# Attention, then two gated feed-forward layers, on one core: fewer filler matmuls in the prologue, and one tile's normalisation split between two engines

## The chip, the core and the metric

One core of a Trainium2 chip runs the whole program in one launch. The metric is device time in microseconds (us) of one execution; lower is better. TensorE (PE) does the matmuls, VectorE (DVE), ScalarE (ACT) and GpSimd (POOL) the work on elements, SyncE's queue (SP) issues nearly all transfers (DMA).

## What is computed

```python
# attention: q, k, v [4, 8, 768, 64], 8 memory keys a head, chunks of 32, 16 left and 8 right
scores = scale * q_c @ concat(mem_k, k_ctx)^T        # 32 x up to 64
a = exp(scores - max); a = a / (sum(a) + 1e-9)
out[chunk] = a @ concat(mem_v, v_ctx)
x = out as [3072, 512]
x = (sigmoid(x @ w_gate) * (x @ w_val)) @ w_out      # d_ff 1536
h = x @ w_in                                         # d_ff 2048
y = (h * sigmoid(1.702 h)) @ w2_out                  # [3072, 512]
```

Inputs and weights are wider than 32 bits where they are weights of the layers; each is converted to a high and a low 32-bit part on the chip, and every layer matmul is done as three (high x high, high x low, low x high).

## The kernel before, in words

Attention is cut into 32 tiles of 96 tokens (three chunks of 32); the layers run over blocks of 512 tokens. The first six tiles (`NPRO` = 6, t = 0 to 5) feed the first block and form the **prologue**: nothing else can be multiplied until their output is there. Each tile goes through the same steps: transposes of q and k on PE (L397, L405), their eviction on ACT (L412, L417, L418), the scores S on PE (L508), maximum and subtraction on DVE (L525, L528), exp on ACT (L536), sum, addition of 1e-9 and reciprocal on DVE (L565, L567, L568), the normalisation (L576: three bands of 32 rows by 448 and one piece of 96 by 64 for the memory keys, written into `pw`), the transpose PT on PE (L598) and its eviction on ACT (L605), the product PV with v on PE (L655), and the split of its result into the high part `xh` on ACT (L687) and the low part `xl` on DVE (L690). In the same stretch the first weights are converted, one unit u at a time: load (L262), rebias on ACT (L266), shift, sign and join on DVE or ACT (L271, L280 or L276, L285), high part on ACT (L290), low part on DVE or GpSimd (L295).

The order of all instructions is made ahead by a planner (`Schedule`): each task has an engine, a planned duration and a due time, and the planner lists tasks in order of planned start. Every engine then works through its own list strictly in order, waiting on semaphores. Only the order is fixed by the plan; on the chip the durations are what they are.

When the planner's list is emitted, `run` puts **filler matmuls** ahead of every PE task of the prologue: wherever the plan has PE waiting, `int(FILL * gap / FILL_US)` products of the identity with itself (L809, 128x128, float32, result never read) are queued, from the time `WAKE` up to the first product of the first layer (L745, `sch.first`). Their number is fixed in the program: they are run whether PE really has to wait at that place or not.

The first layer's products are L745 (high parts) and L752 (low part), with the gate at L769 to L780 and the second matmul at L924; the second layer's are L1231 and L719. After the prologue `open_late` gives the prologue's memory to later buffers: the spare weight buffers `raw_s` and the q and k buffer of tiles 6 to 8 (`qkn_a`) lie there, so their loads wait until the prologue's last reader is done, the fillers' identity tile included.

The normalisation's engines stand in `en` (L590): one name for each of the three bands, and the memory piece goes with band 0. In the kernel before, tiles 0, 2 and 4 have all pieces on GpSimd, the other tiles have band 0 and the memory piece on DVE and two bands on GpSimd.

Of the kernel before, what the change touches and what calls it, by code (L numbers as in the profile page):

```python
# [24 lines left out]
TK = TQ + LEFT + RIGHT  # L25
NEG = -1.0e30
HOP = 0.2
WAKE, FILL, FILL_US = 1.4, 0.8, 0.107
SAME = 0.05


# [92 lines left out]
def c_dve(n, k=1):  # L124
    return k * 0.13 + n / 960.0


def c_act(n):
    return 0.13 + n / 1200.0
# [7 lines left out]
def kernel(  # L137
# [35 lines left out]
    NPRO = len(tiles[0])  # L173
# [179 lines left out]
    def attention(t, bufs, banks, pe_path, extra=None):  # L353
# [9 lines left out]
        def tadd(eng, dur, fn, r=(), w=(), **kw):  # L363
            add(eng, dur, fn, r=r, w=w, slack=SL, **kw)
# [207 lines left out]
        def norm(eng, dst, rows_, keys):  # L572
            r = slice(*rows_)
            c = slice(*keys)
            n = rows_[1] - rows_[0]
            eng.tensor_tensor(  # L576
                out=dst, in0=e3()[r, :, c], in1=T["sm"][r].to_broadcast([n, H, keys[1] - keys[0]]), op=ALU.mult
            )

        if pe_path:  # L580

            def ev_norm(c):
                r = (c * CH, (c + 1) * CH)
                eng = nc.vector if en[c] == "dve" else nc.gpsimd
                norm(eng, T["pw"][r[0] : r[1], :, c * CH : c * CH + CTX], r, (0, CTX))

            def ev_norm_m():
                norm(nc.vector if en[0] == "dve" else nc.gpsimd, T["pw"][:, :, TK:P], (0, TQ), (CTX, KW))

            en = ["pool", "pool", "pool"] if t < NPRO and t % 2 == 0 else ["dve", "pool", "pool"]  # L590
            for c in range(NCK):
                tadd(en[c], 0.75 if en[c] == "dve" else 1.2, lambda c=c: ev_norm(c), r=ke + [kk["sm"]], w=[(kk["pw"], c)])
            tadd(en[0], 0.25 if en[0] == "dve" else 0.35, ev_norm_m, r=ke + [kk["sm"]], w=[(kk["pw"], 3)])

            def pe_pt():
                for h in range(H):
                    a, p = divmod(h, NP)
                    nc.tensor.transpose(  # L598
                        bt[a][:, p * TQ : (p + 1) * TQ], T["pw"][:, h, :], ident()[:TQ, :TQ]
                    )  # L600

            def ev_pt(a):
                src = bt[a][:, : NP * TQ]
                dst = T["pt"].rearrange("p (a h) s -> p a (h s)", a=2)[:, a, :]
                nc.scalar.activation(dst, src, AF.Copy)  # L605

            tadd("pe", 0.7, pe_pt, r=[(kk["pw"], c) for c in range(4)] + [bufs.kid], w=kbt, margin=mg)
            for a in range(2):
                tadd("act", c_act(384), lambda a=a: ev_pt(a), r=[kbt[a]], w=[(kk["pt"], a)])
        else:  # L610

            def ev_norm():
                norm(nc.vector, T["pn"][0:L, :, 3 * CH - NM : 3 * CH], (0, L), (CTX, KW))
                norm(nc.vector, T["pn"][L:TQ, :, CTX:KW], (L, TQ), (CTX, KW))

            tadd(
                "pool",
                0.95,
                lambda: norm(nc.gpsimd, T["pn"][:, :, 0:CTX], (0, TQ), (0, CTX)),
                r=ke + [kk["sm"]],  # L620
                w=[(kk["pn"], 0)],
            )
            tadd("dve", c_dve(128, 2), ev_norm, r=ke + [kk["sm"]], w=[(kk["pn"], 1)])


            PTB = ((0, 0, 0), (1, 0, 1), (2, 0, 2), (0, 1, 1), (1, 1, 2), (2, 1, 3), (0, 2, 3), (1, 2, 3))

            def ev_pt(part):
                for c, kb, r in PTB[4 * part : 4 * part + 4]:
                    nc.vector.transpose(  # L630
                        T["pt"][r * CH : (r + 1) * CH, :, c * CH : (c + 1) * CH],
                        T["pn"][c * CH : (c + 1) * CH, :, kb * CH : (kb + 1) * CH],
                    )

            for part in range(2):
                tadd(
                    "dve",
                    c_dve(1024, 4),
                    lambda part=part: ev_pt(part),
                    r=[(kk["pn"], 0), (kk["pn"], 1)],  # L640
                    w=[(kk["pt"], part)],
                )
# [224 lines left out]
    def attend(ts, bufs, banks):  # L867
        for t in ts:
            attention(t, bufs(t), banks(t), True)
# [37 lines left out]
    def attention_b(b):  # L907
        for t in tiles[b]:
            if t < NPE:
                continue  # L910
            first = t == NPE
            x = pb[(t // 2) % 2 * 2 + t % 2]
            head = first or t % 2 == 0
            attention(t, x, (A0, A1), False, (0 if head else NCK, 2 - t % 2 if head else 0, first or t % TPB == 0))
# [474 lines left out]
```

## Time and profile before

| | |
|---|---|
| median of 3 runs | 1194.86 us (1193.78 to 1195.18) |
| the profiled execution | 1193.88 us, of which its span is 1192.1 us |
| PE busy | 1184.7 us, 99% of the span |
| DVE, ACT, POOL busy | 716.7, 474.7, 80.9 us |
| granted TensorE clock | 1.00 of full speed (2.4 GHz) in every slice |

Matmul records overlap: the sum of durations of a group counts time twice, so the time that a run of matmuls took is read from the chain of work or from start to start. One float32 matmul leaves two records (two passes). "x44" in a row on fillers is thus 22 fillers. Rows are read as start, length, what, count.

### The profile page before, as it was taken

The numbers are of one execution on the slowest core, as the hardware profiler recorded it, in microseconds if no ns is written. First come the engines' busy times: TensorE is split into PE (matmuls) and PEld (weight loads), VectorE is DVE, ScalarE is ACT, GpSimd is POOL, SyncE is SP. The second block draws the span as 40 slices with busy tenths as digits, with TensorE's granted clock in tenths as the row PEclk, the third lists the DMA queues.
The fourth block names the chain that finished last, engine by engine and source line by source line (L and its number), as shares of the span: only waits on it lengthen the run. The fifth ranks groups of instructions, "written<-read, shape, count | busy, mean of one in ns | idle before, by whom it ended". The sixth has DMA issues, their size and how long they took to land.

```text
span 1192.1 us, 19585 instructions
## 1 busy us (share of the span) xinstructions
PE 1184.7 (99%) x7574; PEld 995.2 (83%) x7574; DVE 716.7 (60%) x1465; ACT 474.7 (40%) x832; POOL 80.9 (7%) x82
## 2 busy tenths in 40 slices
PE   9999999999999999999999999999999999999998
PEld 8878889998888888888888888888888888888887
DVE  5699847885478347716874788857333356253342
ACT  4688732222122212212253686746233344243332
POOL 4323310000000000000000100000000000000000
PEclk9999999999999999999999999999999999999999
DMA  9386332233123202301272347645243453244100
GB/s 210 98 251 200 100 79 48 51 58 82 20 47 58 56 17 48 68 14 26 72 258 78 124 148 246 216 159 168 71 124 89 124 150 115 69 126 116 44 36 35
DMA packets 193484, 122.09 MB, mean 102 GB/s; under 512 B 138480, under 2 KB 159216, under 8 KB 193392
## 3 DMA queue, kind: packets, MB, share of 16 engines
q1 hardware_dynamic: 189936, 114.56, 35.3%
q10 hardware_dynamic: 3456, 6.29, 1.4%
q8 instruction: 59, 0.97, 0.4%
q14 instruction: 33, 0.27, 0.1%
HBM read 93.54 MB, written 27.26 MB: 101 GB/s over the span
## 4 chain that ended last, share of the span: by engine, by line
PE 98%; DMA 1%; DVE 0%; ACT 0%; issue 0%; POOL 0%; DVEq 0%; POOLq 0%
PE bank L719 22%; PE bank L745 22%; PE bank L1231 19%; PE bank L924 17%; PE bank L752 11%; PE bank L809 3%; PE bank L655 2%; PE bank L508 2%; DMA raw<-in_moe_w_val_dram 1%; PE bank L598 1%; PE bank L405 0%; PE bank L397 0%; DMA raw_s<-in_moe_w_gate_dram 0%; DVE f L285 0%; ACT sig L769 0%
## 5 line engine op out<-in xcount | busy, mean ns | idle before, releaser
L1231 PE MATMUL bank<-sb_x,sb_r 128*128 128x512 f32 x1008 | 241.0, 389 | 0.0
L745 PE MATMUL bank<-xh,w 128*128 128x512 f32 (+1 forms) x656 | 234.0, 365 | 0.6 <-ACT sig L769 0.5
L745 PE MATMUL bank<-xl,w 128*128 128x512 f32 (+1 forms) x656 | 232.9, 363 | 0.0
L1231 PEld LDWEIGHTS bank<-sb_x,sb_r 128*128 128x128 f32 x1008 | 189.2, 188 | 39.3
L719 PE MATMUL bank<-w,gh 128*128 128x512 f32 x672 | 206.8, 389 | 0.0
L924 PE MATMUL bank<-gh,w 128*128 128x512 f32 (+1 forms) x656 | 158.8, 364 | 0.0
L752 PE MATMUL bank<-xh,w 128*128 128x512 f32 (+1 forms) x656 | 158.3, 366 | 0.0
L719 PEld LDWEIGHTS bank<-w,gh 128*128 128x128 f32 x672 | 126.2, 188 | 26.2
L745 PEld LDWEIGHTS bank<-xh,w 128*128 128x128 f32 x656 | 123.8, 189 | 21.1 <-ACT sig L769 1.2
L745 PEld LDWEIGHTS bank<-xl,w 128*128 128x128 f32 x656 | 123.8, 189 | 19.4
L924 PEld LDWEIGHTS bank<-gh,w 128*128 128x128 f32 x656 | 115.0, 189 | 19.7 <-ACT f L944 0.2
L752 PEld LDWEIGHTS bank<-xh,w 128*128 128x128 f32 x656 | 114.0, 189 | 20.2
L719 PE MATMUL bank<-w,gl 128*128 128x512 f32 x336 | 130.7, 389 | 0.0
L772 DVE SCALAR_TENSOR_TENSOR sig<-sig,bank 128x512 f32<-128x512 f32 (+1 forms) x82 | 50.8, 619 | 106.7 <-PE bank L752 106.1
L777 ACT ACTIVATE gh<-sig 128x512 fp32r<-128x512 f32 (+1 forms) x82 | 47.6, 580 | 161.9 <-DVE sig L772 161.9
L769 ACT ACTIVATE sig<-bank 128x512 f32<-128x512 f32 (+1 forms) x82 | 44.8, 546 | 126.1 <-PE bank L752 123.6
L1247 DVE TENSOR_TENSOR sb_s<-bank,sb_s 128x512 f32<-128x512 f32 x72 | 49.5, 691 | 72.3 <-PE bank L1231 60.4
L630 DVE STREAM_TRANSPOSE pt<-raw 32x256 f32<-32x256 f32 x184 | 80.0, 435 | 2.4
L924 PE MATMUL bank<-gl,w 128*128 128x512 f32 (+1 forms) x328 | 80.7, 368 | 0.0
L719 PEld LDWEIGHTS bank<-w,gl 128*128 128x128 f32 x336 | 63.1, 188 | 13.1
L1243 ACT ACTIVATE sb_s<-bank 128x512 f32<-128x512 f32 x72 | 43.1, 599 | 68.6 <-PE bank L1231 64.7
L1274 ACT ACTIVATE sig<-sb_s 128x512 f32<-128x512 f32 x72 | 45.5, 632 | 59.3 <-DVE sb_s L1247 38.0
(126 smaller groups left out, 1322.4 us busy)
## 6 DMA issues: line engine op xcount, KB each, us to landing
sb_r<-wc_dram SPq DMA_DIRECT2D x112, 256.0 KB
raw<-in_moe_w_out_dram SPq DMA_DIRECT2D x24, 512.0 KB
wc_dram<-sb_r SPq DMA_DIRECT2D x24, 512.0 KB
raw<-in_moe_w_in_dram SPq DMA_DIRECT2D x16, 512.0 KB
y_dram<-f ACTq DMA_DIRECT2D x24, 256.0 KB
out_dram<-f SPq DMA_DIRECT2D x23, 256.0 KB
vn<-in_v_dram SPq DMA_DIRECT2D x24, 240.0 KB
f<-in_q_dram SPq DMA_DIRECT2D x276, 16.0 KB
```

The costliest lines, as they stand in the source:

```text
L630: nc.vector.transpose(T["pt"][r * CH : (r + 1) * CH, :, c * CH : (c + 1) * CH], T["pn"][c * CH : (c + 1) * CH, :, kb * CH : (kb + 1) * CH],)
L719: nc.tensor.matmul(ps_out, a, c, start=(first and i == 0 and j == 0), stop=(last and i == n - 1 and j == 2),)
L745: nc.tensor.matmul(bank[bk][:, :n], w[:, 0, ts[t]], x[xb][:, t, c0 : c0 + n], start=t == 0 and x is xhs, stop=False)
L752: nc.tensor.matmul(bank[bk][:, :n], w[:, 1, ts[t]], xhs[xb][:, t, c0 : c0 + n], start=False, stop=t == NK - 1)
L769: nc.scalar.activation(sig[:, :n], bank[src_sig][:, :n], AF.Tanh, scale=scale / 2)
L772: nc.vector.scalar_tensor_tensor(out=sig[:, :n], in0=sig[:, :n], scalar=1.0, in1=bank[src_val][:, :n], op0=ALU.add, op1=ALU.mult)
L777: nc.scalar.activation(gh[:, :n], sig[:, :n], AF.Copy, scale=0.5)
L924: nc.tensor.matmul(bank[Y[m]][:, c0 : c0 + n], w[:, wi, m * P : (m + 1) * P], g[:, :n], start=f == 0 and j == 0 and c0 == 0, stop=f == F1 ...
L1231: nc.tensor.matmul(bank[bk], w[:, o : o + P], xt[x, k][:, xl, :], start=first and k == 0 and wl == 0 and xl == 0, stop=k == 1 and wl == 1, ...
L1243: add("act", c_act(BLK), lambda: nc.scalar.activation(work[n], bank[bk], AF.Copy), r=[("bank", bk)], w=[n])
L1247: nc.vector.tensor_tensor(out=work[n], in0=bank[bk], in1=work[n], op=ALU.add)
L1274: add("act", c_act(BLK), lambda: nc.scalar.activation(sigs[i], src(), AF.Tanh, scale=0.851), r=[ksrc], w=[ks])
```

## The change

Two edits. The constants that turn a planned wait of PE into fillers: a filler is counted at 0.22 us in place of 0.107, and 0.5 of a wait is filled in place of 0.8. And the engine list of the normalisation: of the prologue's tiles only 0 and 2 keep all pieces on GpSimd; tile 4 gets band 0 and the memory piece on DVE, as the odd tiles have. The plan itself doesn't count fillers, so the order of instructions changes only by the second edit.

```diff
-WAKE, FILL, FILL_US = 1.4, 0.8, 0.107
+WAKE, FILL, FILL_US = 1.4, 0.5, 0.22
@@
-            en = ["pool", "pool", "pool"] if t < NPRO and t % 2 == 0 else ["dve", "pool", "pool"]
+            en = ["pool", "pool", "pool"] if t in (0, 2) else ["dve", "pool", "pool"]
             for c in range(NCK):
                 tadd(en[c], 0.75 if en[c] == "dve" else 1.2, lambda c=c: ev_norm(c), r=ke + [kk["sm"]], w=[(kk["pw"], c)])
             tadd(en[0], 0.25 if en[0] == "dve" else 0.35, ev_norm_m, r=ke + [kk["sm"]], w=[(kk["pw"], 3)])
```

## Rows read from the trace of the kernel before

**Rows 1.** Waits of PE over the whole span (who for whom: us, times, longest)

```profile
PE bank L397 <- DMA qkn_a<-in_q_dram: 1.7, 1, 1.7
PE bank L745 <- ACT sig L769: 0.5, 1, 0.5
```

**Rows 2.** Chain of work that ended last, 0 to 54 us (start, us, what, records)

```profile
1.36 6.93 PE bank L809 x44
...
9.06 2.01 PE bank L809 x18
...
40.62 0.66 PE bank L598 x8
...
45.16 3.15 PE bank L809 x28
48.31 0.81 PE bank L655 x16
49.12 4.00 PE bank L809 x34
```

**Rows 3.** The fillers' line alone, prologue (stretch, length, PE, PEld, clock, DMA, GB/s)

```profile
1.36:53.13 51.77, 34.65 (x270) 32.91 (x270) 1.00 0.68 147
```

**Rows 4.** Timeline of PE where the first product starts

```profile
52.87 0.48 PE L745 MATMUL bank<-xh,w 128*128 128x512 f32 x1
...
60.26 0.52 PE L397 MATMUL bank<-ident_a,qkn_a 96*128 96x96 f32 x4 [1.67 <-DMA qkn_a<-in_q_dram]
```

**Rows 5.** Busy time by stretch (length; PE, PEld, DVE, ACT, POOL; clock, DMA, GB/s)

```profile
8.00:53.00 45.00, 45.00 (x710) 42.21 (x709) 31.83 (x75) 28.52 (x57) 17.05 (x18) 1.00 0.64 138
60.00:80.00 20.00, 19.59 (x90) 15.99 (x91) 17.25 (x29) 16.32 (x27) 2.39 (x2) 1.00 0.86 260
80.00:100.00 20.00, 20.00 (x139) 16.34 (x138) 19.47 (x35) 15.39 (x25) 7.74 (x5) 1.00 0.60 183
100.00:1192.00 1092.00, 1087.85 (x6575) 909.72 (x6573) 641.37 (x1320) 410.46 (x720) 47.26 (x45) 1.00 0.34 95
```

**Rows 6.** Bytes moved in the first 80 us, 40 slices of 2 us

```profile
GB/s 3 221 247 213 175 175 198 185 208 199 215 243 248 343 295 300 40 0 8 240 23 0 0 4 8 0 0 233 352 276 300 306 321 268 360 243 195 231 200 181
```

**Rows 7.** Timeline of ACT, last eviction of tile 0's keys

```profile
9.73 0.24 ACT L418 ACTIVATE kt<-bank 128x96 f32<-128x96 f32 x1
```

**Rows 8.** Timeline of DVE in the prologue

```profile
11.79 0.11 DVE L522 MEMSET bank<- 32x64 f32 x1 [6.64 <-PE bank L508]
...
20.95 1.49 DVE L576 TENSOR_TENSOR pw<-e,sm 32x448 f32<-32x448 f32 x2
...
38.79 0.74 DVE L576 TENSOR_TENSOR pw<-e,sm 32x448 f32<-32x448 f32 x2
...
49.76 0.62 DVE L690 TENSOR_TENSOR xl<-bank,xh 128x256 fp32r<-128x256 f32 x2 [1.98 <-ACT xh L687]
...
50.90 1.88 DVE L295 TENSOR_TENSOR w<-f,w 128x512 fp32r<-128x512 f32 x3
```

**Rows 9.** Waits of DVE, 0 to 53 us

```profile
DVE xl L690 <- ACT xh L687: 5.5, 5, 2.0
DVE sm L565 <- ACT e L536: 2.5, 3, 1.0
```

**Rows 10.** Timeline of POOL: the normalisations of tiles 4 and 5

```profile
33.28 3.95 POOL L576 TENSOR_TENSOR pw<-e,sm 32x448 f32<-32x448 f32 x4 [3.32 <-DVE sm L568]
37.87 3.06 POOL L576 TENSOR_TENSOR pw<-e,sm 32x448 f32<-32x448 f32 x2 [0.64 <-DVE sm L568]
```

**Rows 11.** The chain of rows 2, after the prologue

```profile
53.25 2.51 DMA raw_s<-in_moe_w_gate_dram
...
67.32 2.11 PE bank L745 x8
```

**Rows 12.** The fillers' line by single us (columns as in rows 3)

```profile
3.00:4.00 1.00, 1.00 (x7) 1.00 (x6) 1.00 1.15 258
6.00:7.00 1.00, 1.00 (x11) 1.00 (x10) 1.00 1.15 240
```

## The prediction

> **What bounds the kernel now.** I read the waits of PE first. Over 1192.1 us PE waits 1.7 us once for a load and 0.5 us once for ACT after it has begun [rows 1]: by this view there is nothing to win but PE's own work. So I asked which of that work is wanted. The chain of work that ended last answers for the first 53 us: it runs through PE without a break, and most of its pieces are fillers, L809 [rows 2]. The line alone has 270 records between 1.36 and 53.13 us, that is 135 fillers at two records each [rows 3]. The first 22 take 6.93 us, later ones 2.01 us for 9, so 0.223 us each [rows 2]: with the other 113 at 0.223 that is 6.9 + 25.2 = about 32 us, and the rest of the 51.8 us, about 19.5 us, is wanted work of six tiles. The first product starts at 52.87 us [rows 4], the moment that the last 17 fillers let it (they stand in the chain from 49.12 for 4.00 us [rows 2]), although the last `xl` that it reads was done at 49.76 + 0.62 = 50.38 us [rows 8]. From the first product on PE is busy: 1087.85 of the last 1092 us [rows 5]. So the place of the change is the prologue, and the fillers there are not cover for waits but the bound.
>
> **The fillers, step by step.** A planned gap g gave int(0.8 g / 0.107) = int(7.48 g) fillers, which take 7.48 x 0.223 = 1.67 g: each planned wait was filled to one and two thirds of itself. Now it gives int(2.27 g), or 0.51 g. The counts in the trace tell the gaps: 22 fillers mean g of 2.94 to 3.08 us, so 6 now; 9 give 2 or 3, 14 give 4, 17 give 5. Over the thirteen runs this makes 35 or 36 in place of 135. They cost 36 x 0.223 = 8.0 us, so 24 us leave PE's queue. PE alone would then reach the first product at 1.4 + 19.5 + 8 = 29 us. It will not be the bound; what is late next must be found.
>
> **Next: the loads.** They are issued by SP and don't wait for PE until 26 us into the run, so they land as before. With the bytes of the rows summed in issue order, q and k of tile 0 (0.70 MB moved, the next tile's keys among them) are in by 5.0 us, those of tile 5 (3.28 MB) by 18.1 us [rows 6]; I add 0.5 us for the last packet's receipt, an estimate. PE took up tile 0 at 1.36 + 6.93 = 8.29 us, so 2.8 us after it could have.
>
> **Next: DVE, which I take as the new bound.** Before, its first tile came at 11.79 us [rows 8]. From the start of tile 0's transposes (8.29) to the end of the key eviction (9.73 + 0.24 = 9.97 [rows 7]) is 1.7 us, the scores take 0.67 us of PE; so DVE can begin at 5.5 + 1.7 + 0.7 = 7.9, say 8.0 us. In 8 to 53 us DVE is busy 31.83 us [rows 5] and idle 13.2. Of the idle time 3.8 us lies ahead of 11.79; 5.5 us are waits of `xl` for ACT, which waits for PV behind fillers; 2.5 us are waits of the sum for exp, which follows DVE's own subtraction and can't be filled when only one or two tiles are in work [rows 9]. I keep the 2.5 and let the rest go. Tile 4's band adds 1 us (below). Then all that DVE did by 52.78 us is done by 8.0 + 31.8 + 2.5 + 1.0 = 43.3 us, and the last `xl`, 52.78 - 50.38 = 2.4 us ahead of that in its list [rows 8], at 40.9 us. I put the first product at 41.5 us, with 0.6 us for PV and ACT of tile 5, whose order can't be perfect. The bounds: with no idle time at all 38.4 us; with 7.5 us of idle left, 46 us.
>
> **Tile 4's normalisation.** GpSimd's four pieces took 3.95 us for tile 4, where two bands of tile 5 took 3.06 [rows 10]; two bands cost 2.0 (half of 3.95) to 3.1 us, so POOL is freed by 0.9 to 2 us. DVE gets a band and the memory piece: the row of two such pieces has 1.49 us beside a busy POOL and 0.74 in another place [rows 8]; I take 1.0. What is queued behind them on DVE: shift, sign and join of the first weights and the last `xl`s, thus the new bound, so the 1.0 us counts in full. What POOL gains: tile 5's normalisation waited for DVE and not for POOL (0.64 us, "DVE sm" [rows 10]), and tile 4's transpose came at 40.62 [rows 2], 3.4 us after POOL was done. So alone this edit is worth between -1.9 us (if tile 4's own chain binds) and +1.5 us; +1.0 stands in the sum, by the DVE row. The Trainium skill, "GPSIMD Engine Reference", section "1. Specifications", says that GpSimd shares its SBUF interfaces with VectorE and that they contend when a DVE instruction has two SBUF inputs, as the normalisation has; by that rule the band would cost 1.49 and not 1.0, and the time would be 0.5 us longer. The trace has it both ways, 1.49 and 0.74, each beside a running POOL.
>
> **After the first product.** Two things follow the shift. The loads for tiles 6 to 8 and the spare weights start when the prologue's last reader is done (53.25 us, just after the last filler [rows 11]); tile 6's q came 7.0 us later (60.26, PE waiting 1.67 [rows 4]), and the chain to the product at 67.32 is 14.1 us long from there. Five fillers behind the last PV end at about 40.7 us, so this chain moves by 12.5 us, the first product by 52.87 - 41.5 = 11.4; the smaller counts. DVE is 86 and 97% busy from 60 to 100 us [rows 5], so it must not start that stretch behind: low parts of weights that were done before the first product now end 1.8 us after it, while DVE idled about 4 us for the loads at that place; that covers it, barely. From 100 us on PE has no wait worth naming, and an earlier start goes to the end.
>
> **The sum.** 1193.88 (profiled execution) - 11.4 = 1182.5. That execution lies 1.0 us below the median of the runs shown (1193.78 to 1195.18); for the median of the new kernel I add half of it: **1183.0 us**.
>
> **The rivals.**
> *The gain is partly given back (1186 to 1190).* For it: DVE's 97% in 80 to 100 us, and a list whose order follows planned durations and not real ones. If 5 more of the 13.2 us of idle time stay, the first product comes at 46.5 us and the time is 1188. Against it: these waits are seen to hang on PV and the scores behind fillers.
> *More (below 1180.5).* DVE without idle time: 38.4 us, 14.5 less, 1179.5.
> *No change (1191.5 to 1196).* The lists put something ahead of the last `xl` that comes when it came before, such as a weight whose buffer is freed late. For it: the slices with 240 GB/s at 38 to 40 us show one such reload [rows 6]. Against: its buffer is freed by DVE's own work, which moves ahead.
> *Slower: TensorE's lower clock level.* The granted clock reads 1.00 throughout, but the same filler pass is done 7 times in the us from 3 and 11 times in that from 6, after PE had run without a pause from 1.36 [rows 12]: at the start PE is 1.57 times slower, whatever the clock column says. With 36 fillers PE pauses in every gap. If PE stays slow to the end of the prologue, its work after the first six fillers, 19.5 + 30 x 0.223 = 26.2 us, becomes 41 us at 1.57, so a first product at 5.5 + 41 = 46.6 us (1188), and 52 us at a full factor of 2 (1.2 for 2.4 GHz): 57.9 us, 5 us later than before, some 1199. It decides from a factor of 47.4 / 26.2 = 1.8 on. Against it: slow PE work has no pauses left, so it looks like the stretch from 1.36 that brought the speed up. The Trainium skill, "TensorE: Matmul & The Clock Gate", section "What's actually happening", says that the half-rate clock is the default and that activity releases it; this is the rule that speaks against the change, and by it the fast prologue isn't sure. The first us of the trace agree with it in the pass times; no run here shows a fall.
>
> **How the numbers follow.** Forecast (1180.5 to 1186) 0.70; partly given back 0.15; more 0.06; no change 0.05; slower 0.04. The range takes the bounds of DVE's idle time, 38.4 to 47.5 us for the first product: 1179.5 to 1189.5. About 0.2% (2.4 us) is what a measurement can tell from no change here. Faster 0.91, same 0.05, slower 0.04.
>
> **What the new profile would show.** Some 72 records of L809; the first product at 39 to 44 us; DVE's first tile at 8 to 9 us, and DVE over 90% busy from 20 us to the first product; two POOL pieces for tile 4, PE's wait for tile 6's q no longer than 1.7 us, and the same PE stretch after it. Wrong would be: the first product later than 47 us; DVE with many waits for PE before it; passes of L809 or L508 slow after 10 us; or new waits of PE between 45 and 100 us that add up to more than 3 us.

## The result: 1180.26 us, and where the 13 us of the profile went

| | before | after |
|---|---|---|
| median | 1194.35 us (1193.78 to 1195.18, 4 runs) | 1180.26 us (1179.00 to 1180.80, 4 runs) |
| the profiled execution, its span | 1193.88, 1192.1 us | 1180.80, 1179.0 us |
| fillers | 135 | 33 |
| first product of the first layer | 52.87 us | 40.84 us |
| POOL's two bands of tile 5 | 3.06 us | 3.56 us |

The ratio is 0.988, with a 95% interval of 0.9863 to 0.9897: 1.2% faster. The new profile shows 33 fillers and not the 35 or 36 that the counts of the old one promised, because the second edit shifts the plan a little.

Two kernels' chains can be laid side by side from three points. The first product starts 12.03 us earlier (52.87, 40.84). The first product of the third group, which hangs on the next loads (67.32 [rows 11]), stands at 54.66, 12.66 us earlier. From there to the end the kernels take 1124.78 and 1124.34 us. So 12.0 us are won ahead of the first product, 0.6 from there to the third group (0.4 of them at PE's wait for the next tile's loads, 1.67 and 1.26 us), and 0.4 in all that follows.

The chain of work that ended last, in the prologue of the changed kernel (start, us, what, records). Before, nearly all of it was PE, and most of that fillers [rows 2]:

```profile
7.54 4.65 DMA kn<-in_mem_k_dram
...
14.38 0.77 DVE sm L567
15.14 0.66 DVE e L528 x2
15.80 0.12 DVE sm L568
16.02 1.49 DVE pw L576 x2
...
28.25 1.71 DVE pw L576 x2
29.96 0.60 DVE sm L565
...
32.27 1.42 DVE pw L576 x2
33.72 1.71 POOL pw L576
35.47 1.54 PE bank L598 x8
37.01 1.33 PE bank L809 x6
38.34 1.10 PE bank L655 x16
39.45 1.32 PE bank L809 x10
```

The reader is to see three stretches. Up to 12 us the chain is loads. From 13.65 us to 33.72 it is DVE, almost without a break. After that comes GpSimd, and then PE, slow at first: three fillers (six records) take 1.33 us, where 0.67 us is usual.

The waits of PE over the whole span now stand where the fillers were (who for whom: us, times, longest; compare [rows 1]):

```profile
PE bank L598 <- POOL pw L576: 2.0, 1, 2.0
PE bank L809 <- POOL ident masks.py:199: 1.4, 1, 1.4
PE bank L655 <- ACT pt L605: 1.3, 2, 1.0
PE bank L405 <- DMA qkn_a<-in_mem_k_dram: 1.3, 1, 1.3
PE bank L405 <- DMA kn<-in_mem_k_dram: 1.2, 1, 1.2
```

PE waits more than before and the kernel is faster: what a wait replaces counts, not its length. And the clock column, which was 1.00 throughout, has a dip (stretch, length; PE, PEld, DVE, ACT, POOL busy; granted clock, DMA, GB/s):

```profile
33.00:34.00 1.00, 0.45 (x5) 0.26 (x3) 1.00 (x3) 0.88 (x2) 0.94 (x2) 1.00 0.49 92
34.00:35.00 1.00, 0.00 (x0) 0.00 (x0) 1.00 (x3) 0.95 (x1) 1.00 (x1) 1.00 1.01 347
36.00:38.00 2.00, 2.00 (x13) 2.00 (x11) 1.20 (x3) 1.44 (x4) 0.00 (x0) 0.50 0.00 0
39.00:40.00 1.00, 1.00 (x17) 0.88 (x14) 0.49 (x2) 0.86 (x4) 0.00 (x0) 1.00 0.00 0
```

PE stood still for 2.0 us, waiting for GpSimd's bands of tile 5, and came back at 0.50 (1.2 GHz) for its last transposes, the three fillers behind them and the beginning of the last PV; from 39 us on the column shows 1.00 again.

### The profile page after: what moved, and what is told of

Same layout as the page of the kernel before. It is cut to its first block, busy times and chain, and to the rows that moved or that the text cites. A ratio compares the mean times of both kernels' runs of the same rounds, so it can differ in the third digit from the quotient of the medians.

```text
span 1179.0 us, 19177 instructions
## 1 busy us (share of the span) xinstructions
PE 1165.1 (99%) x7370; PEld 974.2 (83%) x7370; DVE 720.9 (61%) x1467; ACT 475.1 (40%) x832; POOL 82.5 (7%) x80
## 4 chain that ended last, share of the span: by engine, by line
PE 96%; DVE 2%; DMA 1%; SPq 1%; POOL 0%; issue 0%; ACT 0%; DVEq 0%; POOLq 0%
PE bank L719 22%; PE bank L745 22%; PE bank L1231 19%; PE bank L924 17%; PE bank L752 11%; PE bank L655 2%; PE bank L508 2%; SPq L317 1%; DVE pw L576 1%; DMA kn<-in_mem_k_dram 0%; DMA qkn_a<-in_mem_k_dram 0%; PE bank L598 0%; DVE mx L525 0%; PE bank L809 0%; DVE e L528 0%; DVE sm L565 0%
```

## The experiments

Each stands beside runs of the kernel before on the same chip (medians of 1194.17 to 1194.36 us), and the changed kernel was run twice more for comparison. Single executions of one kernel differ by up to 3.0 us here (1193.51 to 1196.50 for the kernel before on one chip), so medians of four under 1 us apart say nothing.

### The changed kernel again, twice

> The changed kernel once more, on the chip and beside the runs of the three kernels below, so that differences of 1 us can be read. Every theory: 1179 to 1181 us, first product near 40.8 us.

> The changed kernel once more as the partner of the two kernels below on their chip. Every theory: 1179.5 to 1181 us; tile 5's pieces on GpSimd near 3.56 us, TensorE at the low clock level for some 3 us around the last transposes (in both looks so far 35.5 to 38.6 us).

Measured: 1180.28 us (1179.25 to 1181.52) and 1180.09 us (1178.95 to 1180.74). The first product stood at 39.30 and 39.45 us, 1.4 to 1.5 us earlier than in the first profile, on the same instructions. The clock differs too: low in the first of them, and not in the second, although PE stood still for 2.02 us in both. In the first it did not fall at once: PE took up its work again at 34.29 us, and the column reads 1.00 until 35 us. The dip, then, isn't fixed by the program.

The first of the two (columns as above), and below it the second:

```profile
36.00:38.00 2.00, 2.00 (x19) 1.71 (x19) 1.41 (x4) 1.91 (x4) 0.00 (x0) 0.50 0.01 4
```

```profile
33.00:35.00 2.00, 0.02 (x1) 0.02 (x1) 2.00 (x5) 1.74 (x3) 1.87 (x2) 1.00 0.83 245
36.00:38.00 2.00, 2.00 (x28) 1.76 (x27) 1.67 (x5) 2.00 (x4) 0.00 (x0) 1.00 0.02 4
```

### The fillers' edit alone

```diff
-WAKE, FILL, FILL_US = 1.4, 0.8, 0.107
+WAKE, FILL, FILL_US = 1.4, 0.5, 0.22
```

> The fillers' edit alone; tile 4's normalisation stays whole on GpSimd, so the order of all instructions is that of the kernel before, with 35 fillers. Theory (fillers were the bound, DVE is the next): first product at 40 to 43 us, time 1180 to 1183 us. By the prediction's sum, tile 4's edit costs 1.0 us of DVE in front of the first product, so this kernel would be 1 us faster than the changed one (first product at 39.8 us where that has 40.84). Rival: the second edit is what lets the order follow; two weight steps of DVE (0.7 us each) stand behind the last xl in the changed kernel and ahead of it here, so this kernel is 0.5 to 1.5 us slower (first product at 41.3 to 42.3 us).

Measured: 1180.26 us (1179.62 to 1180.63), first product at 39.37 us, 35 fillers. This edit alone brings the whole gain. The theory on the fillers holds. Between the 1.0 us faster and the rival's 0.5 to 1.5 us slower it chose neither: the time is that of the changed kernel (1180.26, 1180.28, 1180.09), and its first product lies among the three of that kernel (39.30, 39.45, 40.84).

### Tile 4's edit alone

```diff
-            en = ["pool", "pool", "pool"] if t < NPRO and t % 2 == 0 else ["dve", "pool", "pool"]
+            en = ["pool", "pool", "pool"] if t in (0, 2) else ["dve", "pool", "pool"]
```

> The edit of tile 4's normalisation alone, the fillers counted as before (130 of them, 135 in the kernel before). Theory (PE with its fillers is the bound of the prologue): what counts is the number of fillers, 5 fewer at 0.223 us, so the first product comes about 1.1 us earlier (51.8 us for 52.87) and the time is 1193 us. Rival (tile 4's own chain or DVE is on the path even behind the fillers): 1.9 us faster or 1.5 us slower than before, as the first product's time would show.

Measured: 1192.24 us (1191.82 to 1193.67, 10 runs), ratio 0.9986 with 0.9976 to 0.9995; first product at 52.06 us, 0.81 us earlier. It is 2.1 us faster, where five fillers less make 1.1. The total is near the rival's 1.9 us; the first product, which was to tell the two apart, moved by less than the theory's 1.1. PE has no wait in this prologue but the one at its start, as before, so fillers still bound it, and 0.8 of the first product's time fits the five (the first 22 fillers took 7.20 us there, for 6.93). Where the other 1 us comes from I did not settle: the wait for the next loads is 1.5 us for 1.7, the third group's first product comes 1.16 us earlier (66.16 for 67.32), 0.5 us of the profile's gain of 1.7 lies behind that, and the interval reaches down to 0.6 us.

### No filler at all, and the whole wait filled

```diff
-WAKE, FILL, FILL_US = 1.4, 0.5, 0.22
+WAKE, FILL, FILL_US = 1.4, 0.0, 0.22
```

> The changed kernel without any filler. Theory (half the fillers cost nothing because DVE is the bound): the first product comes at 40 to 41 us as in the changed kernel if the clock stays, and the loads for the next tiles start up to 1.3 us earlier, for 1179 to 1180 us. Rival (the clock): TensorE runs at 1.2 GHz through the prologue; its 19.5 us of wanted work become up to 39 us, the first product comes 2 to 5 us later and the first 24 products of 512 columns take up to 0.43 us each for 0.227: 1183 to 1190 us.

Measured: 1183.94 us (1183.10 to 1184.79), first product at 43.23 us. The rival's time was right, at the low end of its range, but the low level did not last through the prologue: the column shows it for some 10 us, from shortly before 38 to 48 us. The busy times by stretch (columns as above):

```profile
20.00:37.00 17.00, 13.31 (x227) 10.92 (x226) 14.92 (x38) 13.18 (x29) 9.77 (x11) 1.00 0.78 212
37.00:46.00 9.00, 6.37 (x31) 5.03 (x32) 7.81 (x17) 7.83 (x13) 2.61 (x4) 0.53 0.46 150
46.00:60.00 14.00, 14.00 (x61) 11.49 (x60) 11.38 (x18) 10.22 (x18) 4.96 (x3) 0.93 0.86 249
```

And products at the low level, in its PE timeline (start, us):

```profile
45.08 0.63 PE L745 MATMUL bank<-xh,w 128*128 128x512 f32 x1
45.50 0.63 PE L745 MATMUL bank<-xl,w 128*128 128x512 f32 x1
...
48.66 0.39 PE L745 MATMUL bank<-xh,w 128*128 128x512 f32 x1
48.89 0.39 PE L745 MATMUL bank<-xl,w 128*128 128x512 f32 x1
```

From start to start they are 0.42 us apart at the low level and 0.23 at the high one. At the beginning, too, everything is slow: the first k transposes take 1.06 us there and 0.63 in the changed kernel, although the clock column says 1.00 from 5 to 37 us. It doesn't show the slow start that [rows 12] showed either; the records of the matmuls do.

```diff
-WAKE, FILL, FILL_US = 1.4, 0.5, 0.22
+WAKE, FILL, FILL_US = 1.4, 1.0, 0.22
```

> The changed kernel with the whole planned wait filled (a filler counted at 0.22 us as before, 74 fillers for 36). Theory A (DVE and GpSimd set the pace; fillers that fit the wait cost little): 38 more fillers are 8.5 us of PE, most of it in waits; the first product comes 0 to 3 us later, clock at 2.4 GHz throughout, total 1179 to 1183 us. Theory B (each filler over half a wait delays the chain in full): first product 8 us later, 1188 us.

Measured: 1183.82 us (1181.82 to 1184.76), first product at 42.04 us. Neither theory has it right: no low clock in the prologue (theory A), but 3.5 us lost against the changed kernel on the same chip, between A's 0 to 3 and B's 8. Part of it came after the prologue. In this profile, the slowest of the four executions, the identity was released later, the next loads with it, and PE waited 2.40 us for them and fell to the low level in turn:

```profile
50.16 0.69 PE L405 MATMUL bank<-ident_a,qkn_a 128*128 128x128 f32 x4 [2.40 <-DMA qkn_a<-in_mem_k_dram]
50.55 0.74 PE L745 MATMUL bank<-xh,w 128*128 128x512 f32 x1
51.08 0.63 PE L745 MATMUL bank<-xl,w 128*128 128x512 f32 x1
```

By the number of fillers, then: none 1183.9, 28 (below) 1179.7, 33 to 35 1180.3, 74 1183.8, 135 1194.4 us.

### More work on DVE

```diff
-        tadd("dve", 0.12, lambda: nc.vector.reciprocal(T["sm"], T["sm"]), w=[kk["sm"]])
+        def ev_recip():
+            nc.vector.reciprocal(T["sm"], T["sm"])
+            if t < NPRO:
+                for _ in range(2):
+                    nc.vector.memset(pad0, 0.0)
+
+        tadd("dve", 0.12, ev_recip, w=[kk["sm"]])
```

> The changed kernel with two needless memsets of 128x224 on DVE behind the reciprocal of each of the six prologue tiles, some 0.25 us each by size from the 0.91 us of a 96x1024 one, so about 3 us more work on DVE; order and fillers unchanged. Theory (DVE is the bound of the new prologue): the first product comes 2 to 3 us later (43 to 44 us) and the time is 1182 to 1183.5 us. Rival (GpSimd, PE with its low clock, or the loads set the end, DVE has slack): under 1 us later.

Measured: 1180.21 us (1179.54 to 1180.85), first product at 40.53 us: the rival's "under 1 us". The twelve memsets took 3.6 us (0.60 a pair), and the median shows no cost; the first product is 1.1 to 1.2 us later than in the two further profiles of the changed kernel and 0.3 earlier than in its first one. In this profile, too, the clock fell, and earlier: to 0.50 from 31 to 33 us, after PE had waited 1.78 us until 29.45. The timelines of DVE and POOL show why the work cost so little. First the changed kernel:

```profile
12.63 0.68 DVE L565 TENSOR_REDUCE sm<-e 96x8 f32<-96x512 f32 x1 [0.59 <-ACT e L536]
...
16.02 1.49 DVE L576 TENSOR_TENSOR pw<-e,sm 32x448 f32<-32x448 f32 x2
...
28.18 1.78 DVE L576 TENSOR_TENSOR pw<-e,sm 32x448 f32<-32x448 f32 x2
...
31.85 3.56 POOL L576 TENSOR_TENSOR pw<-e,sm 32x448 f32<-32x448 f32 x2 [1.97 <-DVE sm L568]
```

and then the kernel with memsets (its L582 is L576):

```profile
12.76 0.60 DVE L572 MEMSET pad<- 128x224 f32 x2
13.35 0.68 DVE L565 TENSOR_REDUCE sm<-e 96x8 f32<-96x512 f32 x1
...
16.16 0.78 DVE L582 TENSOR_TENSOR pw<-e,sm 32x448 f32<-32x448 f32 x2
...
29.27 1.01 DVE L582 TENSOR_TENSOR pw<-e,sm 32x448 f32<-32x448 f32 x2
...
32.17 2.27 POOL L582 TENSOR_TENSOR pw<-e,sm 32x448 f32<-32x448 f32 x2 [2.50 <-DVE sm L569]
```

Three effects hide them. A pair fills DVE's wait for exp (0.59 us ahead of the sum in the one, none in the other). And a pair shifts DVE's two pieces against GpSimd's bands: these take 0.78 and 1.01 us in place of 1.49 and 1.78, and GpSimd's bands of tile 5 take 2.27 in place of 3.56. And near the end DVE waits less for ACT: 0.92 us ahead of a weight and 0.59 ahead of the last `xl` in the changed kernel, 0.20 us in all here. DVE's busy time holds time that comes from the other engine's work beside it, which a small shift takes away. What decides it is open: the pieces of tile 5 in the same kernel take 1.48 us still. The Trainium skill, "GPSIMD Engine Reference", section "1. Specifications", says that the two engines contend where a DVE instruction has two SBUF inputs; the trace agrees as far as it goes (both operands of L576 are in SBUF), and adds the price, here up to 1.9 times on DVE and 1.6 times on GpSimd. But the 0.78 us stood beside a running band too. In the run below that leaves GpSimd idle beside tile 5, DVE did all four pieces in 2.10 us, where two took 1.48 beside the bands. That bears contention out for this tile; what lets other pieces pass was not tried.

### Less work on DVE

```diff
-        tadd("dve", 0.07, lambda: nc.vector.tensor_scalar_add(T["sm"], T["sm"], 1e-9), w=[kk["sm"]])
+        tadd("dve", 0.07, lambda: nc.vector.tensor_scalar_add(T["sm"], T["sm"], 1e-9) if t >= NPRO else None, w=[kk["sm"]])
```

> The changed kernel without the six additions of 1e-9 to the sums of the prologue's tiles (L567; a part of the computation that is left out, six instructions of DVE that took 1.9 us together in the changed kernel); order and fillers unchanged. Theory A (DVE bounds the new prologue up to tile 5's reciprocal): that reciprocal ends 1 to 1.9 us earlier (31.7 us now) and the first product 1 to 1.9 us earlier (40.84 now), for 1178.5 to 1179.5 us. Theory B (DVE has slack; the path is loads and TensorE): less than 0.4 us in both.

Measured: 1178.21 us (1177.93 to 1180.22) beside 1180.28 for the changed kernel on the same chip; tile 5's reciprocal at 30.26 us, first product at 38.67. Against the first profile (31.53, 40.84) that is 1.3 and 2.2 us, against the run beside it (30.36, 39.30) 0.1 and 0.6. The median favours theory A; the profile beside it doesn't decide, since its clock fell and the other's didn't, and since its first scores came 0.8 us earlier (6.40 for 7.20). The second further profile of the changed kernel, on another chip, had the clock at 1.00 as this one and its first scores at 7.13: against it (31.05, 39.45) both are 0.8 us earlier. So the same was taken from the kernel with the fillers' edit alone:

> The fillers' edit alone (tile 4 whole on GpSimd), without the six additions of 1e-9 in the prologue. Theory A (DVE's list is a bound of the new prologue, whatever the split of tile 4): the additions are worth here what they were in the changed kernel, 1 to 2 us: 1178.3 to 1179.3 us for 1180.26 with them, first product at 38 to 38.8 us. Theory B (the gain there was chance, or belongs to tile 4's split): 1179.9 to 1180.6 us.

Measured: 1179.45 us (1178.92 to 1180.63), first product at 38.53 us: 0.8 us of the median and of the first product, between the two theories (on another chip than the kernel with them). That the additions cost something, some 0.8 us of the first product, is likely from these two pairs of profiles, and not shown by the medians, whose ranges overlap.

### The last leg: tile 5 on DVE, and the last fillers

```diff
-            en = ["pool", "pool", "pool"] if t in (0, 2) else ["dve", "pool", "pool"]
+            en = ["pool", "pool", "pool"] if t in (0, 2) else ["dve"] * 3 if t == NPRO - 1 else ["dve", "pool", "pool"]
```

> The changed kernel with all four normalisation pieces of the last prologue tile, 5, on DVE and none on GpSimd; the plan's order shifts a little by it, 41 fillers. Theory A (the last leg of the prologue is GpSimd's 3.56 us for two bands, slowed by DVE beside it, and TensorE's 2.0 us wait for it, in which the clock falls): DVE does the four pieces in 1.3 to 2.2 us without contention, the last transposes come 1 to 1.5 us earlier, the clock stays, the first product comes 1 to 2 us earlier: 1178.5 to 1179.5 us. Theory B (DVE is still the bound there): its list gets 0.7 to 1.4 us longer, the first product comes up to 1 us later: 1181 us.

Measured: 1180.28 us (1179.27 to 1180.52) for 1180.09 beside it. The four pieces took 2.10 us on DVE, the last transposes came at 33.72 us (34.98 beside it), the clock stayed (as it did beside it), all as theory A had it; but the first product came at 39.34 us (39.45) and not 1 to 2 us earlier, and the time is neither theory's. What is late next is a weight:

```profile
33.72 0.88 PE L598 MATMUL bank<-ident,pw 96*128 96x96 f32 x8 [0.66 <-DVE pw L576]
...
39.34 0.47 PE L745 MATMUL bank<-xh,w 128*128 128x512 f32 x1 [0.78 <-ACT w L290]
```

ACT's high part of the first weights ends last. So several chains end within 1 us of each other in front of the first product, and shortening one of them brings nothing.

> The kernel with tile 5's normalisation on DVE, and without the six additions of 1e-9 in the prologue (left out as in the run without the additions, which had 1178.2 us). Theory A (GpSimd's last leg and DVE's length both count): 1177 to 1178 us, first product at 37.5 to 38.5 us. Theory B (only DVE's length counts): 1178 to 1179 us.

Measured: 1179.13 us (1178.17 to 1179.62), first product at 38.81 us: just above theory B's range. Of all kernels here the changed one without the additions, which leaves out a part of the computation, is the fastest at 1178.21 us; it beats the kernel before clearly, the changed kernel by 2.1 us of the median with ranges that overlap.

For the last fillers, those between the last PV and the first product are left out:

```diff
-            if T[i]["eng"] == "pe" and end is not None:
+            if T[i]["eng"] == "pe" and end is not None and i != self.first:
```

> The changed kernel without the five fillers between the last PV and the first product; the other 31 stay. Theory A (loads for the next tiles start when the last filler is done, and TensorE waits for them after its first 24 products): they start 1.2 us earlier, the wait of 1.26 us for them all but goes, the first product stays at 40.7 us, total 1.2 us less than the changed kernel. Theory B (the clock): the pause ahead of the first product leaves TensorE at 1.2 GHz, its products take 0.43 us for 0.227, and 2 to 4 us are lost.

28 fillers are left. Measured: 1179.72 us (1179.70 to 1180.60) for 1180.28. Both theories came true in part. The loads were issued at 37.74 us (39.68 beside it) and PE had no wait for them (1.66 us beside it). But the first product waited 2.07 us for the last `xl`, the clock fell, and eight of its products ran at the low level:

```profile
39.67 0.47 PE L746 MATMUL bank<-xh,w 128*128 128x512 f32 x1 [2.07 <-DVE xl L691]
...
41.50 0.63 PE L746 MATMUL bank<-xh,w 128*128 128x512 f32 x1
```

The gain of 1.7 us at the loads was paid back by the products. The clock had fallen once before in this profile, to 0.50 from 31 to 33 us, after PE's waits of only 1.00 us until 28.21 and 0.38 until 29.85.

## Why the prediction was right, point by point

**The bound.** That fillers held the prologue is shown by the fillers' edit alone, which brings the whole gain (1180.26 us). The old view of waits (2.2 us in all) could not have told it; the chain did.

**The count.** 35 or 36 fillers were forecast: 35 with that edit alone, 33 with both. PE alone was to reach the first product at 29 us; it came to 40.84 with PE no longer the bound, as said.

**The loads.** The forecast was 5.5 us for tile 0's q and k; q was there at 4.45 and k by 4.97. No row shows the 0.5 us that I added for the receipt, and the 5.0 of the bytes alone would have fitted. For later tiles I saw no wait for loads, and that was wrong: PE waited 1.2 us until 12.3 us for tile 3's memory keys (0.9 and none in the two other profiles), a small transfer that SP issues last of the tile's q and k, at 7.54 us. The bytes of [rows 6] would have had them in at 10.7 us.

**DVE's sum.** Forecast: a start at 8.0, 31.8 + 1.0 - 2.4 = 30.4 us of work and 2.5 of idle time ahead of the end of the last `xl`, so 40.9. Measured in the first profile: a start at 7.35, 29.4 us of work, 3.9 of idle time, 40.70. The end fits by luck: the terms are each off by about 1 us and cancel, and in the two further profiles the first product came at 39.30 and 39.45 us, 2 us ahead of the 41.5. Of the work, two weight steps (0.7 us each) went behind the last `xl` by the new order, and tile 4's pieces took 1.78 us where I had taken 1.0; of the idle time 1.9 are the waits for exp that I had kept and 1.5 are waits for ACT at the end that I had not seen.

**DVE as the bound.** Only half true, and the step that failed is "so the 1.0 us counts in full". The chain runs on DVE from 13.65 to 33.72 us; but 3.6 us more on it left the median as it was in the run with memsets, since they fell into its waits for exp and ACT and shortened its pieces beside GpSimd's. And the last 7 us belong to GpSimd's bands, PE at the low clock, ACT's weights and `xl` together. Tile 4's edit, priced at +1.0, is worth nothing measurable beside the new fillers, inside the bounds of -1.9 to +1.5. Of the two prices for its pieces the dearer one, 1.49, was the better: 1.78 in the trace.

**After the first product.** The next loads were to start 12.5 us earlier; they start at 40.89 for 53.25, 12.4. PE's wait for them was to be no longer than 1.7 us; it is 1.26. I took the smaller of two shifts (11.4 of 12.5), but the product that hangs on the loads moved by 12.66. From there on nothing was lost: the feared stretch from 60 to 100 us has PE busy 40.00 of 40.00 us.

**The clock.** I gave its lowest level 0.04 as the cause of a slower kernel, and priced it for the whole prologue. It did fall, in two of three profiles of the changed kernel, for one short stretch, and with it came one of the signs that I had named for being wrong, slow passes of fillers after 10 us (1.33 us for 0.67 at 37 us). Without fillers, where the low level shows longest, the loss is 3.7 us and the kernel is still 10 us faster than before. The fall to 1188 or 1199 us was mis-sized: the low level shows there for some 10 us and not for the whole prologue. By the chains the slow stretches of PE also lie partly under DVE's work and under the wait for the loads; how much that hides was not measured. The Trainium skill, "TensorE: Matmul & The Clock Gate", section "What's actually happening", has activity release the half rate; the runs agree in kind (0.50 after pauses of PE, 1.00 again behind more work).

**The sum.** 1183.0 us were forecast and 1180.26 measured. The profiled executions say 1182.5 and 1180.8: 0.7 us of the difference is the first product (41.5, 40.84), 0.6 the stretch with the wait for loads, 0.4 the rest. The other 1 us is the step from the profiled execution to the median: I added 0.5, and the profiled one of the new kernel was 0.5 above its median. So the median lies in the range of 1179.5 to 1189.5, but 0.24 us below the band of 1180.5 to 1186 that I gave 0.70, in the one of "more" that I gave 0.06; that rival's mechanism, DVE without idle time, did not come (3.9 us of idle). The upper end of the range was badly worked out: by the rows 7.5 us of idle time make 46 us and not 47.5, and by the sum 38.4 and 47.5 us make 1179.4 and 1188.5.

## What to carry to other kernels

A filler is only free while the wait that it fills is real: in the program its number is fixed, and on an in-order engine every filler that comes too many delays the work behind it. Its cost has to be measured (0.223 us here, planned at 0.107), and then there is a best in between: too few leave the engine at half speed for part of the time (1183.9), too many queue in front of the work (1183.8 and 1194.4). When a busy engine shows no waits, read which of its work is wanted.

## What the runs showed of the hardware

- DVE and GpSimd, each multiplying two operands from SBUF at the same time: DVE's pair of pieces took 0.74 to 1.79 us by where it fell against GpSimd's bands, and GpSimd's pair 1.93 to 3.56. A needless pair of memsets of 0.60 us, by shifting one against the other, partly paid for itself.
- The granted clock fell to 0.50, at most 1.2 us after PE's pause had ended, where PE had stood still for 2.0 to 2.9 us (tile 5's bands, the next loads, the last `xl`) or for 1.78 us (with memsets), and once, without the last fillers, where the pauses shortly before were 1.00 and 0.38 us. It did not fall in two other profiles with a pause of 2.02 us, nor after the 1.67 us in the kernel before; the same program had it in two of three profiles. The length of the last pause alone doesn't decide.
- The clock column doesn't show the slow start: 1.00 is printed while fillers and transposes take 1.5 times as long and more.
